# Strassen's products moved from the third matmul of a gated feed-forward to its first two, in half of the tokens

## Chip, core and metric

The kernel runs on one core of a Trainium2 chip. A core has five engines that run their own instruction streams and wait for each other through semaphores: TensorE (PE, matmuls, with weight loads counted apart as PEld), VectorE (DVE), ScalarE (ACT), GpSimd (POOL) and SyncE (SP, which only issues DMAs here). Matmul results land in PSUM, in banks of 512 float32 columns; everything else lives in SBUF. The metric is the device time of one execution in microseconds, as the median of several runs; lower is better.

## What is computed

```python
def _A_ref(x, wqkv, wo):            # B, S, D = 1, 2048, 512
    H = 32; Dh = D // H; W = 256
    qkv = (x @ wqkv).reshape(B, S, 3, H, Dh).transpose(2, 0, 3, 1, 4)
    q, k, v = qkv[0], qkv[1], qkv[2]
    scores = jnp.einsum("bhqd,bhkd->bhqk", q, k) * (Dh ** -0.5)
    mask = (idx[:, None] - idx[None, :] >= 0) & (idx[:, None] - idx[None, :] < W)
    p = softmax(jnp.where(mask, scores, -1e9))
    return einsum("bhqk,bhkd->bhqd", p, v) ... @ wo

def _B_ref(x, w1, w3, w2):          # F = 1792
    gate = jnp.einsum("bsd,df->bsf", x, w1)
    up = jnp.einsum("bsd,df->bsf", x, w3)
    return jnp.einsum("bsf,fd->bsd", silu(gate) * up, w2)

xn = layernorm(x)
return x + _A_ref(xn, wqkv, wo) * silu(_B_ref(xn, w1, w3, w2))
```

All inputs are float32.

## The kernel before

**Precision.** Each large matmul works in float16 with an operand split in a high and a low half, so a product is three matmuls: high by high, high by low, low by high. Splitting costs a cast (ScalarE or GpSimd) and a subtraction (GpSimd or VectorE). Weights are scaled by powers of two first.

**Tiles and units.** The 2048 tokens are four tiles of 512 (`t` from 0 to 3). Attention is done for 4 groups of 8 heads a tile, in two halves each, which gives 32 units. A unit has five batches of attention matmuls (`PLAN`): scores of the unit itself (`W`, line 720, followed by mask additions on VectorE, line 726, and an exponential on ScalarE, line 728), scores of a later unit for the row maxima (`M`, `X`, `N`, line 637, reduced on VectorE, line 650), and in the last batch the values (line 746). Between batches stand gaps, which are filled with dense matmuls.

**Dense work.** These are the projections of queries and keys (`project`, line 572), values (`value`, 539), the feed-forward, and the output product with the final gating (`total`, 1273). The feed-forward's hidden width of 1792 is 14 blocks of 128 (`f`). `gate_up(t, f)` makes 12 matmuls for gate and 12 for up, 512 columns each (line 1004), a Tanh on ScalarE (1018) and two VectorE products with PSUM (1021, 1025). In tiles 0 and 1 `down` (1224) multiplies by w2, in groups of 4, 4, 3 and 3 blocks, for 4 blocks of 128 tokens each, and adds groups in SBUF (1246).

In tiles 2 and 3 Down is a Strassen product: two blocks of `f` form a pair, tokens are split by parity and the output columns in half. `fold_weights` makes sums of quarters of w2 during tile 1 and stores them in `dFold`; `fold_first` and `fold_second` make sums of the hidden values on GpSimd and split them (1056 to 1084); `fold_down_piece` runs seven products of 256 columns (1144), and `unfold` adds them up (on GpSimd in tile 2, on VectorE in tile 3, lines 317 and 1176).

**Order.** `feed_forward` gives a list of pieces with costs (in units of one 512-column matmul). `more` takes from it so that each unit gets an equal share, and `spread` deals it over the gaps in proportion. Program order is kept on TensorE (`ORDERED`). For VectorE, ScalarE, GpSimd and SyncE the tables in `QUEUES` name the order of instructions by number, and `TURNS` lists pairs of a VectorE instruction that some GpSimd instruction has to wait for.

**Buffers.** Dense products use two PSUM banks in turn (`bank`, names m0 and m1). Scores have two buffers of two banks (`s`), and values and some scores share one of two banks (`po`). In SBUF 54 slots of 2 KB a partition are taken and given (`take`, `give`), and a slot given is reused.

Of the kernel before, what the change touches and what calls it, by code (L numbers as in the profile page):

```python
# [21 lines left out]
P = 128  # L22
# [16 lines left out]
XS = 2.0**10  # L39
# [4 lines left out]
HS = 2.0**4  # L44
# [7 lines left out]
SLOTS = 54  # L52
ORDERED = {ENGINE.PE}
GROUPS = ((0, 4), (4, 8), (8, 11), (11, 14))
FOLDS = ((0, 4), (4, 7))
FOLD_AT = (0, 1, 3, 5, 7, 9, 11)
SEVEN = (0, 6, 3, 4, 5, 1, 2)
KINDS = ((0,), (6, 3), (4, 5), (1, 2))
# [22 lines left out]
def tile_block(ctx: ExitStack, tc: tile.TileContext, x, wqkv, wo, w1, w3, w2, out):  # L81
# [17 lines left out]
    fpool = pool("fpool", 2)  # L99
    psm = pool("psm", 1, PSUM)  # L100
# [51 lines left out]
    open_bank = [0]  # L152

    def bank(shape, dtype=F32):

        open_bank[0] = b = 1 - open_bank[0]
        return psm.tile(shape, dtype, name=f"m{b}", tag=f"m{b}", bufs=1)
# [60 lines left out]
    dFold = dram.tile([len(KINDS), P, FB // 2, 2 * D], F16, name="dFold")  # L218
# [106 lines left out]

    WQ = {}
# [3 lines left out]
    def weights(name, w):  # L330
# [16 lines left out]
        def cut(apart=0):  # L347
            if name == "wo":

                made = [take(F16) for _ in range(NC)]  # L350
                hi, lo = ([m[:, k * D:(k + 1) * D] for m in made] for k in range(2))
            else:
                both = [const.tile([P, NC, D], F16, name=f"{name}{k}") for k in "hl"]
                hi, lo = ([b[:, c, :] for c in range(NC)] for b in both)
# [170 lines left out]
    def value(j, scores_bank=False):  # L525
# [4 lines left out]
        def part(half):  # L530
# [9 lines left out]
            if half:  # L540
                nc.scalar.activation(V[:, j % VB, 0:H * VW].rearrange("p (h w) -> p h w", w=VW)[:, :, 0:DH],
                                     pv.rearrange("p (h d) -> p h d", d=DH), AF.Copy, scale=sc["uv"])
        return opening([(6, lambda h=h: part(h)) for h in range(2)])
# [278 lines left out]
    sg_scale = const.tile([P, FB], F32, name="sgs")  # L822
    p13 = const.tile([P, FB], F32, name="p13")
# [16 lines left out]
    def measure(f, apart=0, until=8):  # L840
# [4 lines left out]
        def scale(s=None):  # L845
            pp = small.tile([P, 2, 2], F32, name="pp")
            pi = small.tile([P, 2, 2], F32, name="pi")
# [3 lines left out]
        def rest(pp, pi):  # L851
# [5 lines left out]
            def cut(i, k):  # L857
# [3 lines left out]
                split_pool(a[:, 0:D], a[:, D:], raws[i][k], pi[:, k, i:i + 1])  # L861
# [17 lines left out]
    def load_down(t, f):  # L879
        if t:  # L880
            WF[t, f][1] = b = take(F16)
            nc.sync.dma_start(b, dW2[f])
            return
# [3 lines left out]
    def measure_down(k, f):  # L887
# [18 lines left out]
        def rest(p2):  # L906
# [5 lines left out]
            if k:  # L912
                nc.vector.tensor_max(fold_q, fold_q, q)
            else:
                nc.vector.tensor_copy(fold_q, q)
# [14 lines left out]
            if f1 == FB:  # L930
                later(4, fold_scales)
        beside_scores(2, scale)

    fold_q = const.tile([P, 1], F32, name="fq")
    fold_down = const.tile([P, 1], F32, name="fd")
    fold_w = const.tile([P, FB], F32, name="fw")
    folded = []

    def fold_scales():

        folded.append(0)
        nc.vector.tensor_scalar(fold_down, fold_q, 1.0 / (HS * WS), None, op0=ALU.mult)
        nc.vector.reciprocal(fold_q, fold_q)
        nc.vector.tensor_scalar(fold_w, p13, fold_q, WS, op0=ALU.mult, op1=ALU.mult)

    def fold_weights(j):

        cell = {}
        l, r = slice(0, 256), slice(256, 512)
        sub = nc.gpsimd.tensor_sub  # L950

        def load():
            cell["raw"] = [take(F32) for _ in range(2)]
            for i, raw in enumerate(cell["raw"]):
                nc.sync.dma_start(raw, w2[(2 * j + i) * P:(2 * j + i + 1) * P, :])

        def sums():
            assert folded
            e, o = cell["raw"]
            for i, raw in enumerate((e, o)):  # L960
                nc.scalar.activation(raw, raw, AF.Copy, scale=fold_w[:, 2 * j + i:2 * j + i + 1])
            cell["z"] = z, y = [take(F32) for _ in range(2)]
            sub(z[:, l], e[:, r], e[:, l])
            sub(z[:, r], o[:, r], z[:, l])
# [801 lines left out]
```

## Time and profile before

| | |
|---|---|
| median of 3 runs | 799.32 us (798.89 to 800.25) |
| the profiled execution | 798.36 us, span 796.5 us |
| granted TensorE clock, mean | 0.999 |
| HBM read, written | 91.23 MB, 36.57 MB |

The span is the time from the first to the last instruction of the profiled execution. Times in the profile are in microseconds, or ns where it says so. A row of a group has the source line, the engine, the operation, output and inputs, shapes, and after x the count; then the busy time in all and the mean of one in ns; then the idle time ahead of them and who ended it. A row of the timeline has start, duration, and the same names. A row of a stretch has the busy time of PE, PEld, DVE, ACT and POOL with counts, the granted clock, the share of DMA time and GB/s. A matmul's own duration (380 ns at 512 columns) is longer than the distance from its start to the next one's, as matmuls overlap.

### The profile page before, as it was taken

Reading aid. Unit: us, or ns where it says so; the run is one execution under the profiler, and the core shown is the slowest. Engines: PE = TensorE matmul, PEld = TensorE weight load, DVE = VectorE, ACT = ScalarE, POOL = GpSimd, SP = SyncE. Lnnn points to the kernel's source line nnn. Section 1 sums busy time; section 2 is a strip of 40 time slices with the busy share of each in tenths; the row PEclk is TensorE's granted clock in tenths of the full one; section 3 lists DMA queues with packets and bytes.
Section 4 is the critical chain, followed back from the end, with each engine's and each line's share of the span. In section 5 each row is a group of like instructions: output and inputs, shape, how many; then the busy total and the mean of one; then the engine's idle time right before and its main releaser. Section 6 shows DMA issues by size and latency. Waiting matters only on the chain.

```text
span 796.5 us, 23974 instructions
## 1 busy us (share of the span) xinstructions
PE 788.6 (99%) x9181; PEld 403.3 (51%) x9181; DVE 616.6 (77%) x2005; ACT 396.1 (50%) x592; POOL 381.3 (48%) x746
## 2 busy tenths in 40 slices
PE   9999999999999999999999999999999999999997
PEld 4444455444544444444445454466544744466464
DVE  8689998977898678778978887766667877874437
ACT  8789958835365464344343444344434344444411
POOL 2254738742439463277422456330446277640770
PEclk9999999999999999999999999999999999999999
DMA  9878764747565574758465633765463553335431
GB/s 284 219 224 260 237 214 121 250 112 232 170 201 180 180 219 121 230 141 293 122 207 185 174 116 103 185 167 155 142 158 97 152 164 101 89 94 159 138 77 65
DMA packets 109858, 134.18 MB, mean 168 GB/s; under 512 B 18928, under 2 KB 64944, under 8 KB 109744
## 3 DMA queue, kind: packets, MB, share of 16 engines
q1 hardware_dynamic: 109456, 132.13, 55.9%
q8 instruction: 72, 1.18, 0.7%
q10 hardware_dynamic: 288, 0.52, 0.2%
q14 instruction: 42, 0.34, 0.1%
HBM read 91.23 MB, written 36.57 MB: 160 GB/s over the span
## 4 chain that ended last, share of the span: by engine, by line
PE 94%; DVE 3%; DMA 2%; ACT 1%; issue 0%; SPq 0%; DVEq 0%
PE m L1004 38%; PE po L746 9%; PE m L572 9%; PE m L1224 9%; PE m L1144 8%; PE s L720 6%; PE m L1273 5%; PE m L539 5%; PE s L637 3%; PE po L637 2%; DMA slot<-in_A_wqkv_dram 1%; DMA slot<-in_A_x_dram 0%; PE s L488 0%; DMA slot<-in_B_w_dram 0%; DVE junk L232 0%
## 5 line engine op out<-in xcount | busy, mean ns | idle before, releaser
L1004 PE MATMUL m<-XH,slot 128*128 128x512 f16 x896 | 267.3, 380 | 0.0
L728 ACT ACTIVATE pt<-s,es 128x1024 f32<-128x1024 f32 x152 | 167.2, 1114 | 142.7 <-DVE s L726 133.8
L1004 PEld LDWEIGHTS <-slot 128*128 128x128 f16 x1344 | 124.9, 98 | 154.1 <-issue 11.7
L1004 PE MATMUL m<-XL,slot 128*128 128x512 f16 x448 | 169.8, 379 | 0.0
L726 DVE TENSOR_TENSOR s<-s,MK 128x256 f32<-128x256 f32 (+2 forms) x280 | 120.5, 438 | 59.8 <-PE s L720 50.0
L650 DVE CUSTOM_DVE_ANT_0 junk<-s,MW 128x320 bf16<-128x320 f32 x276 | 122.0, 485 | 18.0 <-PE s L637 16.9
L317 POOL TENSOR_TENSOR slot<-slot,slot 128x256 f16<-128x256 f32 (+1 forms) x86 | 58.7, 699 | 75.1 <-ACT slot L1034 30.4
L323 POOL TENSOR_TENSOR slot<-slot,slot 128x128 f16<-128x128 f32 x168 | 66.7, 433 | 45.9 <-ACT slot L321 45.3
L1224 PE MATMUL m<-slot,slot 128*128 128x512 f16 x336 | 78.5, 380 | 0.0
L650 DVE CUSTOM_DVE_ANT_0 junk<-po,MW 128x320 bf16<-128x320 f32 x172 | 77.5, 484 | 0.0
L746 PE MATMUL po<-pt,V 64*32 64x320 f32 (+4 forms) x2880 | 77.2, 342 | 0.0
L1018 ACT ACTIVATE slot<-m,sgs 128x512 f32<-128x512 f32 x56 | 38.4, 686 | 69.2 <-PE m L1004 69.0
L572 PE MATMUL m<-XH,slot 128*128 128x512 f16 x240 | 70.8, 380 | 0.0
L1144 PE MATMUL m<-slot,slot 128*128 128x256 f16 x588 | 68.3, 273 | 0.0
L1059 POOL TENSOR_TENSOR slot<-slot,slot 128x256 f16<-128x256 f32 x98 | 65.1, 672 | 1.8
L1144 PEld LDWEIGHTS <-slot 128*128 128x128 f16 x588 | 56.2, 98 | 11.1 <-issue 2.7
L746 PEld LDWEIGHTS po<-pt,V 64*32 64x32 f32 x2880 | 50.3, 106 | 22.3 <-issue 0.8
L720 PE MATMUL s<-qa,KA 50*64 50x320 f16 (+3 forms) x1472 | 58.0, 259 | 0.0
L1021 DVE SCALAR_TENSOR_TENSOR slot<-slot,m 128x512 f32<-128x512 f32 x56 | 38.3, 683 | 25.2 <-ACT slot L1018 24.9
L572 PEld LDWEIGHTS <-slot 128*128 128x128 f16 x392 | 36.5, 98 | 42.0 <-issue 1.0
L720 PEld LDWEIGHTS <-KA 50*64 50x64 f16 x1472 | 30.0, 105 | 51.5 <-issue 40.0
L1025 DVE SCALAR_TENSOR_TENSOR slot<-m,slot 128x512 f32<-128x512 f32 x56 | 38.6, 689 | 18.7 <-PE m L1004 18.1
(194 smaller groups left out, 1126.2 us busy)
## 6 DMA issues: line engine op xcount, KB each, us to landing
slot<-dW SPq DMA_DIRECT2D x98, 256.0 KB
slot<-in_B_w_dram SPq DMA_DIRECT2D x56, 256.0 KB
slot<-dFold SPq DMA_DIRECT2D x48, 256.0 KB
dW<-slot SPq DMA_DIRECT2D x42, 256.0 KB
slot<-in_A_x_dram SPq DMA_DIRECT2D x30, 256.0 KB
KA<-dK SPq DMA_DIRECT2D x24, 288.0 KB
slot<-dWQ SPq DMA_DIRECT2D x24, 256.0 KB
qa<-dQ SPq DMA_DIRECT2D x30, 192.0 KB
```

What stands on the lines that cost most here:

```text
L317: op(out[:, c], a[:, c], b[:, c])
L323: nc.gpsimd.tensor_sub(lo[:, c:c + P], raw[:, c:c + P], hi[:, c:c + P])
L572: nc.tensor.matmul(cell["pp"][:, cols[n]], w[:, (a * NC + c) * P:(a * NC + c + 1) * P], b[:, c, cols[n]], start=n == 0 and (c, i) == parts ...
L650: nc.vector.tensor_tensor_reduce(out=junk[:, :n], in0=s[:, r, :n], in1=mask, scale=1.0, scalar=NEG, op0=ALU.add, op1=ALU.max, accum_out=M[ ...
L720: nc.tensor.matmul(s[64 * h:64 * h + 64, r, o:o + 64 * n], ka[rows, 2 * p + a, 64 * (m + 4):64 * (m + 5)], qa[rows, 2 * p + a, 64 * (m + k ...
L726: nc.vector.tensor_add(v, v, MK[:, kind, of:of + n, :].unsqueeze(1).to_broadcast([P, 2 * len(which), n, 64]))
L728: nc.scalar.activation(pt, s, AF.Exp, scale=es)
L746: nc.tensor.matmul(cell["po"][32 * i:32 * i + 32, h, 64 * (m + k):64 * (m + k + n)], V[64 * h:64 * h + 64, (4 * t + m // 2) % VB, hd * VW: ...
L1004: nc.tensor.matmul(cell[k], w[:, (a * NC + c) * P:(a * NC + c + 1) * P], b[:, c, :], start=c == 0 and i == 0, stop=c == NC - 1 and i == 2)
L1059: nc.gpsimd.tensor_sub(lo, view, hi)
L1144: nc.tensor.matmul(cell["ps"][:, c], made[:, f:f + P], wj[:, g:g + 256], start=j == j0 and c == 0 and n == 0, stop=j == j1 - 1 and n == 2, ...
L1224: nc.tensor.matmul(ps, hh[:, a * TW + b * P:a * TW + (b + 1) * P], w[:, c * D:(c + 1) * D], start=f == f0 and i == 0, stop=f == f1 - 1 and ...
```

## The change

Strassen's products are taken from Down and used for gate and up of tiles 2 and 3. Down of these tiles is done as in tiles 0 and 1. A pair of blocks `j` (blocks 2j and 2j+1) is one `quad`: the 2x2 split is over the two blocks, the two halves of the model width (256 each), and the two halves of the tile's tokens (256 each). Each of the seven products is 6 matmuls of 256 columns for gate and 6 for up, side by side in one bank (line 1113 in the new kernel). Four of them (p1, p6, p5, p3) add up in one bank, which keeps its sum from one to the next, so that ScalarE copies the sum after each; the other three go through the other bank and are added to a copy by VectorE. While the first bank is retained, `bank` hands out only the other one, to projections, values, Down and totals too.

Sums of quarters of w1 and w3 (`weight_sums`, GpSimd) are made during tile 1 and early in tile 2 from the weights read again, and stored in `dSum`; sums of quarters of the tokens (`token_sums`, GpSimd) near the end of tile 1 and of tile 2. The gating now reads copies in SBUF: product of gate and up on GpSimd, Tanh on ScalarE, one VectorE product, each in two halves of 256.

```diff
-SLOTS = 54
+SLOTS = 51
-FOLDS = ((0, 4), (4, 7))
+QUAD_FROM = 2
+QUAD_AT = ((1, 4), (1, 6), (1, 8), (1, 10), (1, 12), (2, 0), (2, 2))
+HALVES_AT = {2: (1, 11), 3: (2, 5)}
+FIRST_PAIR = 16
+REST = (19, )
+WEIGHTS = (0.9, 1, 1, 1.2, 0.9)
...
     def bank(shape, dtype=F32):
-        open_bank[0] = b = 1 - open_bank[0]
+        open_bank[0] = b = 1 - (open_bank[0] if retained[0] is None else retained[0])
...
-    def fold_weights(j):
-    def fold_first(t, j):
-    def fold_second(t, j):
-    def fold_down_piece(t, k, i):
-    def unfold(t):
+    def in_halves(made, raw):
+        for c in (0, 256):
+            nc.gpsimd.tensor_copy(made[:, c:c + 256], raw[:, c:c + 256])
+            nc.gpsimd.tensor_sub(made[:, 512 + c:768 + c], raw[:, c:c + 256], made[:, c:c + 256])
+    def weight_sums(j):
...
+        def sums(k):
+            a, b = cell[k]
+            add(b[:, r], b[:, l], b[:, r])
+            sub(b[:, l], a[:, l], b[:, l])
+            sub(a[:, l], b[:, r], a[:, l])
+            sub(a[:, r], a[:, r], a[:, l])
...
+    def quad(t, j):
...
+        def product(ps, w, x, first):
+            for k in range(2):
+                for c in range(2):
+                    for n, (a, b) in enumerate(((0, 0), (1, 0), (0, 1))):
+                        nc.tensor.matmul(ps[:, 256 * k:256 * k + 256], w(k, a, c), x(b, c), ...)
+        def copied(ps):
+            made = cpool.tile([P, 512], F32, name="copy")
+            nc.scalar.activation(made, ps, AF.Copy, scale=CS)
+            return made
+        def added(ps, other):
+            nc.vector.scalar_tensor_tensor(other, ps, CS, other, op0=ALU.mult, op1=ALU.add)
+            return other
+        def activated(f, half, made):
...
+            def tangent():
+                nc.gpsimd.tensor_mul(made[:, 256:512], made[:, 0:256], made[:, 256:512])
+                nc.scalar.activation(h, made[:, 0:256], AF.Tanh, scale=sg_apart[:, f:f + 1])
+            def gated():
+                nc.vector.scalar_tensor_tensor(h, h, 1.0, made[:, 256:512], op0=ALU.add, op1=ALU.mult)
+        def p1():
+            cell["a"] = bank([P, 512])
+            retained[0] = open_bank[0]
+            product(cell["a"], plain(0), tokens(0, 0), True)
+            cell["p1"] = copied(cell["a"])
+        def p2():
+            ps = bank([P, 512])
+            product(ps, plain(1), tokens(1, 0), True)
+            activated(e, 0, added(ps, cell["p1"]))
+        def p6():
+            product(cell["a"], summed_up(0, 0), token_sum(1, 256), False)
+            cell["u2"] = copied(cell["a"])
+        def p5():
+            product(cell["a"], summed_up(1, 256), token_sum(0, 0), False)
+            cell["v5"] = copied(cell["a"])
+        def p7():
+            cell["b"] = bank([P, 512])
+            product(cell["b"], summed_up(1, 0), token_sum(0, 256), True)
+            activated(o, 1, added(cell["b"], cell["v5"]))
+        def p3():
+            product(cell["a"], summed_up(0, 256), tokens(1, 256), False)
+            retained[0] = None
+            activated(e, 1, copied(cell["a"]))
+        def p4():
+            product(cell["b"], plain(2), token_sum(1, 0), False)
+            activated(o, 0, added(cell["b"], cell["u2"]))
...
+        return [pieces[:2], pieces[2:3], pieces[3:5], pieces[5:]]
```

From unit 16 on `by_gaps` deals the dense work. The four runs of a pair stand at fixed places: p1 and p2 in the last gap of a unit, p6 in the first gap of the next, p5 and p7 in the second, p3 and p4 in the third. Whole groups of the other dense work (a projection, a value product, a Down or total product) are dealt to the gaps that are left, at most one beside p6 and at most one in the second gap. There are 14 pairs for the last 16 units; unit 19 starts none. `QUEUES` and `TURNS` are new throughout.

In the next two blocks ScalarE's rows stand for one unit of tile 2: the middle of it, from the exponential of its first batch. Before, m_10031, m_10250 are gate products, m_10184 a projection, m_10305 a value product:

```order
L728 ACTIVATE pt<-s,es_1002 128x1024
L1056 CAST slot_10179<-slot_10124 128x256 x2
L728 ACTIVATE pt<-s,es_1002 128x1024
L587 ACTIVATE slot_10241<-m_10184 128x512
L1018 ACTIVATE slot_10266<-m_10250,sgs 128x512
L728 ACTIVATE pt<-s,es_1002 128x1024
L541 ACTIVATE V<-m_10305,uv 128x32x16
```

Now, where m_9939 is the bank retained by a pair and m_10020 a projection in the shared bank:

```order
L740 ACTIVATE pt<-s,es_1004 128x1024
L1119 ACTIVATE copy<-m_9939 128x512
L599 ACTIVATE slot_10033<-m_10020 128x512
L740 ACTIVATE pt<-s,es_1004 128x1024
L1119 ACTIVATE copy<-m_9939 128x512
L1136 ACTIVATE slot_10115<-copy,sga 128x256
L740 ACTIVATE pt<-s,es_1004 128x1024
L1119 ACTIVATE copy<-m_9939 128x512
```

A copy of the retained bank now stands between each two exponentials, and the next product of the pair waits for it.

VectorE's rows at the second and third batch of the same units, from the cast for the maxima on. Before, L1021 gates m_10250:

```order
L679 CAST mt<-s 32x128
L726 TENSOR_TENSOR s<-s,MK 128x4x64
L726 TENSOR_TENSOR s<-s,MK 128x2x2x64
L1021 SCALAR_TENSOR_TENSOR slot_10266<-slot_10266,m_10250 128x512
L650 ISA junk,M<-s,MW 128x320
L650 ISA M 128x1
```

Now, where m_10101 is the shared bank with p7:

```order
L691 CAST mt<-s 32x128
L1123 SCALAR_TENSOR_TENSOR copy<-m_10101,copy 128x512
L738 TENSOR_TENSOR s<-s,MK 128x4x64
L662 ISA junk,M<-s,MW 128x320
L662 ISA M 128x1
L738 TENSOR_TENSOR s<-s,MK 128x2x2x64
```

The sum for p7 now stands ahead of the third batch's masks, and a reduction between the two masks. The rows ahead of these, for the second batch, are a mask, the eviction of m_10020, a mask and four reductions.

VectorE's rows at the end of the program, while TensorE does its last products with w2. Before, L1160 evicts folded products, L317 and L1176 add them up, L811 makes the low half of the last attention output:

```order
L1160 SCALAR_TENSOR_TENSOR slot_12898<-m_13592,fd,slot_12898 128x512
L317 TENSOR_TENSOR slot_12898<-slot_12898,slot_12566 128x256 x2
L811 TENSOR_TENSOR slot_13589<-on,slot_13589 128x512
L1160 SCALAR_TENSOR_TENSOR slot_12925<-m_13612,fd,slot_12925 128x512
L317 TENSOR_TENSOR slot_12604<-slot_12604,slot_12898 128x256 x2
L1176 TENSOR_TENSOR slot_13653<-slot_12604,slot_12667 128x256
```

Now, where L1244 evicts plain Down and L823 is the old L811:

```order
L1266 SCALAR_TENSOR_TENSOR slot_14125<-slot_14125,slot_12572 128x512
L1266 SCALAR_TENSOR_TENSOR slot_14085<-slot_14085,slot_12808 128x512
L1244 SCALAR_TENSOR_TENSOR slot_12996<-m_14060,dsc,slot_12996 128x512
L1244 SCALAR_TENSOR_TENSOR slot_13225<-m_14071,dsc,slot_13225 128x512
L823 TENSOR_TENSOR slot_14057<-on,slot_14057 128x512
L1266 SCALAR_TENSOR_TENSOR slot_14106<-slot_14106,slot_13225 128x512
```

The small adds of the unfolding are gone from the end.

More of the change, by code (lines that the diff above doesn't have):

```diff
@@ L43 @@
 OS = 2.0**9
-HS = 2.0**4
+HS = 2.0**3
+CS = 2.0**-21
 TERMS = 3
@@ L347, in cut @@
         def cut(apart=0):
[L348 to L354, printed above, removed]
+            made = [take(F16) for _ in range(NC)]
+            SQ[name, "slots"] = made
+            hi, lo = ([m[:, k * D:(k + 1) * D] for m in made] for k in range(2))
             def one(c, raw):
@@ L930, in rest @@
             if f1 == FB:
-                later(4, fold_scales)
+                later(4, scales_apart)
         beside_scores(2, scale)
[L934 to L944, printed above, removed]
@@ L1166, in unfold @@
-    def unfold(t):
-        q = [QS7.pop((t, i)) for i in range(7)]
-        add = nc.gpsimd.tensor_add if t < NT - 1 else nc.vector.tensor_add
-        for b in range(4):
-            ACC[t, b] = take(F32)
-        def into(e, d, x, y):
-            for c in range(2):
-                h = slice(256 * c, 256 * c + 256)
-                add(ACC[t, 2 * c + e][:, 256 * d:256 * d + 256], x[:, h], y[:, h])
-        def first():
-            halves(add, q[5], q[5], q[0])
-            halves(add, q[6], q[6], q[5])
-        def second():
-            into(1, 0, q[6], q[3])
-            into(1, 1, q[6], q[4])
-        def third():
-            into(0, 0, q[0], q[1])
-            halves(add, q[5], q[5], q[4])
-            into(0, 1, q[5], q[2])
-            give(*q, after=30)
-            summed.update((t, b) for b in range(4))
-        if t == NT - 1:
-            first()
-            second()
-            third()
-        else:
-            for n, f in enumerate((first, second, third)):
-                later(1 + 4 * n, f)
@@ new lines, in tile_block, with token_sums, both, sums @@
+    HALF = {}
+    def token_sums(t):
+        assert turned[t] == 4
+        xh, xl = X[t]
+        add, sub = nc.gpsimd.tensor_add, nc.gpsimd.tensor_sub
+        l, r = slice(0, 256), slice(256, 512)
+        whole = [take(F32) for _ in range(NC)]
+        HALF[t] = [None] * NC
+        def both(c):
+            halves(add, whole[c], xh[:, c, :], xl[:, c, :])
+        def sums(c):
+            a, b = whole[c], whole[2 + c]
+            sub(a[:, l], a[:, r], a[:, l])
+            sub(a[:, r], b[:, r], a[:, r])
+            sub(b[:, r], b[:, r], a[:, l])
+            sub(b[:, l], b[:, l], b[:, r])
+        def cut(c):
+            HALF[t][c] = made = take(F16)
+            in_halves(made, whole[c])
+            give(whole[c], after=20)
+        n = 0
+        for f, cs in ((both, (0, 2, 1, 3)), (sums, (0, 1)), (cut, (0, 2, 1, 3))):
+            for c in cs:
+                later(n, lambda f=f, c=c: f(c))
+                n += 2
@@ L1312, in total_by_columns, with is_open, in_groups @@
         give(y, xr)
+    def is_open(pieces):
+        return bool(pieces) and hasattr(pieces[-1][1], "opens")
+    def in_groups(pieces):
+        groups = []
+        for piece in pieces:
+            if groups and is_open(groups[-1]):
+                groups[-1].append(piece)
+            else:
+                groups.append([piece])
+        return groups
     def feed_forward():
@@ L1574, in tile_block @@
     want = EARLY
+    coming = []
     for n, u in enumerate(units):
+        for f in ahead[n]:
+            later(5, f)
         if n == 0:
@@ L1597, in tile_block @@
         residual(NT - 1, b)
-    run(ffn)
+    run([piece for group in in_line + coming for piece in group])
     flush()
```

407 lines of the change are left out of this document (205 added, 202 removed), and 207 rows, old and new, of tables (QUEUES, TURNS).

## The prediction

> **What bounds the kernel now.** I read the page first, then who waits for whom on TensorE, then the counts by line and shape, then the order of time in one unit of tile 2.
>
> ```profile
> span 796.5 us, 23974 instructions
> PE 788.6 (99%) x9181; PEld 403.3 (51%) x9181; DVE 616.6 (77%) x2005; ACT 396.1 (50%) x592; POOL 381.3 (48%) x746
> PE 94%; DVE 3%; DMA 2%; ACT 1%; issue 0%; SPq 0%; DVEq 0%
> PE s L539 <- DVE wvl L312: 1.4, 2, 1.0
> PE m L1495 <- DVE onesb L183: 1.0, 1, 1.0
> PE m L468 <- DVE slot L452: 0.5, 1, 0.5
> PE s L265 <- DVE sb L242: 0.2, 1, 0.2
> 500.00:640.00 140.00, 140.00 (x1776) 79.58 (x1775) 101.31 (x324) 55.85 (x71) 52.89 (x90) 1.00 0.55 149
> 640.00:765.00 125.00, 125.00 (x1527) 67.01 (x1526) 81.20 (x234) 53.26 (x71) 73.31 (x123) 1.00 0.40 118
> ```
>
> TensorE's share of the chain is 94%. A busy 99% alone proves little, since ends of matmuls are modelled, but the four rows of waits are all that TensorE's matmuls have: 3.1 us, all in the first 30 us. In the stretches of tiles 2 and 3 (the last two rows) TensorE is never idle, at a granted clock of 1.00; VectorE is busy for 101.31 of 140 us (72%), ScalarE 40%, GpSimd 38 to 59%. So before the change a column streamed less is time saved, one for one, and the others have room on average.
>
> How long a column takes is read where matmuls of one kind stand alone, at the end:
>
> ```profile
> 762.30 0.60 PE L1004 MATMUL m<-XH,slot 128*128 128x512 f16 x2
> 767.49 13.92 PE L1144 MATMUL m<-slot,slot 128*128 128x256 f16 x126
> 781.25 7.93 PE L1273 MATMUL m<-slot,slot 128*128 128x512 f16 x36
> 789.02 2.78 PE L1307 MATMUL m<-slot,slot 128*128 128x256 f16 x24
> ```
>
> From start to start: 36 matmuls of 512 columns in 789.02 - 781.25 = 7.77 us, 215.8 ns each; 126 of 256 columns, each with new weights, in 781.25 - 767.49 = 13.76 us, 109.2 ns each. Two halves cost 1.2% more than one whole.
>
> **The matmuls that go and come.**
>
> ```profile
> L1004 PE MATMUL m<-XH,slot 128*128 128x512 f16 x896 | 267.3, 380 | 0.0
> L1004 PE MATMUL m<-XL,slot 128*128 128x512 f16 x448 | 169.8, 379 | 0.0
> L1224 PE MATMUL m<-slot,slot 128*128 128x512 f16 x336 | 78.5, 380 | 0.0
> L1144 PE MATMUL m<-slot,slot 128*128 128x256 f16 x588 | 68.3, 273 | 0.0
> ```
>
> Gate and up have 896 + 448 = 1344 matmuls over four tiles; the half of tiles 2 and 3 goes: 672 x 215.8 ns = 145.0 us. The folded Down of these tiles goes too: 588 x 109.2 ns = 64.2 us. Plain Down, as tiles 0 and 1 have it, comes: 336 x 215.8 ns = 72.5 us. The Strassen products come: 2 tiles x 7 pairs of blocks x 7 products x 12 = 1176 matmuls of 256 columns, 128.4 us. Sum: 128.4 + 72.5 - 145.0 - 64.2 = **-8.3 us**. The count of batches, and so of the breaks between dense work and attention, stays. If a short run costs what 24 matmuls in 2.78 us say (115.8 ns, with the fill of the last), the 588 matmuls more of this width cost 3.9 us more; I take 109.2, as the products stand inside long runs.
>
> [...]
>
> **The other engines' work.**
>
> ```profile
> L1025 DVE SCALAR_TENSOR_TENSOR slot<-m,slot 128x512 f32<-128x512 f32 x56 | 38.6, 689 | 18.7 <-PE m L1004 18.1
> L1021 DVE SCALAR_TENSOR_TENSOR slot<-slot,m 128x512 f32<-128x512 f32 x56 | 38.3, 683 | 25.2 <-ACT slot L1018 24.9
> L1246 DVE SCALAR_TENSOR_TENSOR slot<-m,dsc,slot 128x512 f32<-128x512 f32 x24 | 17.8, 744 | 4.1 <-PE m L1224 4.1
> L1160 DVE SCALAR_TENSOR_TENSOR slot<-m,fd,slot 128x512 f32<-128x512 f32 x14 | 10.5, 748 | 7.3 <-PE m L1144 7.3
> L1018 ACT ACTIVATE slot<-m,sgs 128x512 f32<-128x512 f32 x56 | 38.4, 686 | 69.2 <-PE m L1004 69.0
> L1059 POOL TENSOR_TENSOR slot<-slot,slot 128x256 f16<-128x256 f32 x98 | 65.1, 672 | 1.8
> L1058 POOL CAST slot<-slot 128x256 f16<-128x256 f32 x56 | 22.5, 408 | 1.3 <-DVE slot L1268 0.7 <-DVE NM L667 0.2
> q1 hardware_dynamic: 109456, 132.13, 55.9%
> ```
>
> VectorE loses 28 each of L1025 and L1021, the 14 of L1160 and 16 small adds of the last unfolding (0.42 us), 55.6 us; it gains 24 evictions of plain Down at 0.744, 42 sums of a product with a copy, priced by the same row, and 56 half-width gatings (some 0.45 us by half a wide row and its start): 74.3 us. That is +18.7 us, 81% of the new span. ScalarE gains 56 copies of products at 0.69, 56 half-width Tanh and 28 scalings of weights against what folding took: some +42 us, 56%. GpSimd gives up all folding (about 200 us by counts at 0.67 to 0.75 and 0.41) and gets weight sums, token sums and gating for about 220. Some 43 transfers of 256 KB more, 11 MB on 132, lift the queue's 55.9% to about 60%. By these sums alone all of it lies beside TensorE's work, and I cost it at nothing. The cover is thin only where order binds.
>
> **Where it binds: the two short gaps of a unit.** While a pair of blocks is open, one of the two banks for dense work stays with it (products 1, 6, 5, 3), and all else shares the other. And p5 with p7, and p3 with p4, stand alone between batches: 24 half-wide matmuls, 2.62 us.
>
> ```profile
> 576.61 0.41 PE L720 MATMUL s<-qa,KA 50*64 50x320 f16 x8
> 577.07 0.90 DVE L726 TENSOR_TENSOR s<-s,MK 128x256 f32<-128x256 f32 x2 [0.97 <-PE s L720]
> 577.23 0.39 PE L539 MATMUL m<-wvh,XH 128*128 128x512 f16 x1
> 578.09 1.12 ACT L728 ACTIVATE pt<-s,es 128x1024 f32<-128x1024 f32 x1 [0.69 <-DVE s L726]
> 578.47 0.48 DVE L650 CUSTOM_DVE_ANT_0 junk<-s,MW 128x320 bf16<-128x320 f32 x1
> 578.88 0.49 DVE L650 CUSTOM_DVE_ANT_0 junk<-s,MW 128x320 bf16<-128x320 f32 x1
> 582.51 0.64 PE L720 MATMUL s<-qa,KA 50*64 50x320 f16 x24
> 587.21 0.47 PE L637 MATMUL s<-KA,qa 48*32 48x320 f16 x16
> ```
>
> Now batches start 5.9 and 4.7 us apart (576.61, 582.51, 587.21). A batch itself takes 577.23 - 576.61 = 0.62 us and 0.1 of break, so the new period of the two short gaps is 0.72 + 2.62 = 3.34 us. I walk VectorE's row in the order shown above from the second batch of a unit on, with t = 0 where that batch starts. First mask at 0.46 (577.07 - 576.61); masks and reductions 0.41 each from start to start (578.88 - 578.47); wide evictions 0.61 to 0.69. Mask, eviction of the group that shares the bank, mask, four reductions, the cast for the maxima (0.2), the sum for p7 (0.66): VectorE is done with the second batch at 4.4. The third batch began at 3.34 and its mask could have begun at 3.8, so VectorE is 0.6 late. Mask, reduction, mask: 5.62. The exponential starts 0.12 later and takes 1.12: 6.86. The fourth batch's scores want that buffer at 2 x 3.34 = 6.68. TensorE stands for about **0.2 us**; with the printed means in place of the pitches it is 0.5, and in a unit where the shared group is evicted by ScalarE it is nothing. Queued behind that matmul on TensorE stands everything dense. The fourth gap (two 2.6 us groups) then gives VectorE its time back, so lateness doesn't add up from unit to unit. The other waits of that kind have more room: p4 needs the sum for p7, done at 4.4, and starts at 3.34 + 0.72 + 1.31 = 5.4; p3 needs ScalarE's copy of p5, which stands behind one exponential, done near 3.9, and starts at 4.06. That one is almost as tight. Bounds: 0 and 0.5 us for each of 14 pairs, 0 to 7 us; I take 0.2, the walk by pitches, nearest to the rows: **+2.8 us**.
>
> **Data on time.** The first p5 of tile 2 needs the token sums, about 90 GpSimd instructions after the last reader of their slots, 56.5 us by the rows above; TensorE has 79 us of work between the two. Cost nothing, 22 us of cover, less what GpSimd waits for DMAs.
>
> **The end.**
>
> ```profile
> 762.41 0.69 DVE L760 COPY os<-po 128x512 f32<-128x512 f32 x1 [1.79 <-DMA slot<-dFold]
> 776.03 1.41 POOL L317 TENSOR_TENSOR on<-on,rb 128x256 f32<-128x256 f32 x2 [1.06 <-DMA rb<-de]
> 778.98 0.68 DVE L811 TENSOR_TENSOR slot<-on,slot 128x512 f16<-128x512 f32 x1
> ```
>
> The last head group's normalised output is ready at 779.66, 17.4 us after the last dense gap begins (762.30). There the old kernel puts 18.95 us of dense work, the new one eight groups of 9 matmuls, 15.5 us, and the product that needs the low half comes 11 matmuls on, at 17.9. So the shorter tail stays covered by half a microsecond. What goes there is in the counts already.
>
> **Sum.** -8.3 + 2.8 = -5.5 us. The profiled execution took 798.36 us, its span 796.5 and 1.86 around it; the median shown is 799.32, 0.96 above. On the profiled run: 792.9; on the median, which is compared: **793.8**. A measurement of this kernel tells about 0.2% from no change, 1.6 us.
>
> **Rivals.**
> 1. VectorE is late by the printed means, 0.5 us a pair: 799.32 - 8.3 + 7.0 = 798.0. For it: 72% busy before and the walk's 0.2 to 0.5. Against: units whose shared group is evicted by ScalarE have slack. Chance 0.17.
> 2. Slower: the shared bank. If evictions stand behind reductions, p5, p4 or the group behind p6 waits on the bank as well. Break-even is 8.3 / 14 = 0.59 us a pair; one more eviction late (0.69) on top of 0.2 gives 0.89, 12.5 us: 803.5. For it: p3's 0.16 us of margin above. Against: the waits overlap, since a late TensorE gives the others time. Chance 0.14.
> 3. Token sums late at tile 2 by a quarter of their cover, 5 us once: 798.8. Chance 0.05.
> 4. The clock. [...] Chance 0.02.
> 5. That it doesn't do what it says: 256-column matmuls would have to take 336 x 215.8 / 588 = 123.3 ns for no gain; 126 in a row took 109.2. Within case 1's time, no chance of its own.
>
> The forecast, 791 to 796.5, has the other 0.62. **Faster** by over 0.2% (below 797.7): 0.62 and half of case 1, 0.70. **Within**: the other half and most of case 3, 0.14. **Slower** (above 800.9): 0.16. The range goes from 790.0, no stall at all (791.0) and the end a little shorter, to 800.5, both upper bounds (7.0 us of stalls and half of the 3.9 for short runs); above it lie cases 2 and 4.
>
> **What will show it.** L1113 at 109 ns from start to start in runs of 24; waits of TensorE for ScalarE's exponential at L732 near 0.2 us in the fourth batch of a unit; span near 791. A wait at L1113 for L1123 or L1119 speaks for case 2, a single long one at the first token sums for case 3, a clock below 1.00 for case 4. The prediction is wrong if TensorE's waits in tiles 2 and 3 sum to over 8 us, or if the first 500 us, in which TensorE's work stays the same, move by more than 1 us.

## The result, and the profile after

The change makes the kernel slower. Its median is 809.06 us (804.34 to 813.65, six runs) against 799.27 us (798.14 to 800.25) for the kernel before on the same chip, a ratio of 1.012 with a 95% interval of 1.0076 to 1.0165. The prediction, 793.8 us with a range of 790.0 to 800.5, misses it by 15 us, on the other side. The profiled execution took 812.34 us, the second longest of the six, with a span of 810.6, 14.1 more than before; the medians differ by 9.8.

The page's first lines after, its chain by engine and its queue, in the order in which they were shown of before:

```profile
span 810.6 us, 24698 instructions
PE 788.5 (97%) x9433; PEld 431.3 (53%) x9433; DVE 617.6 (76%) x2037; ACT 430.9 (53%) x656; POOL 399.3 (49%) x761
q1 hardware_dynamic: 129712, 142.23, 58.7%
PE 55%; DMA 9%; SPq 4%; POOL 2%; DVE 2%; issue 1%; ACT 1%; POOLq 0%; DVEq 0%; ACTq 0%
```

Busy times give no alarm: VectorE has 1 us more than before (the sum had said 18.7; the busy time counts rows that overlap once, and the durations of all its rows, added up, grow by 13.2), ScalarE 34.8 more (42), the queue is at 58.7% (60). But TensorE's share of the chain has fallen from 94% to 55%. Who TensorE waits for (us in all, times, the longest), the first six rows:

```profile
PE m L1113 <- DMA slot<-dW: 4.6, 1, 4.6
PE m L1113 <- DMA slot<-dSum: 4.1, 1, 4.1
PE m L1113 <- ACT copy L1119: 3.1, 1, 3.1
PE s L649 <- ACT pt L740: 2.4, 4, 0.7
PE m L1540 <- DVE onesb L188: 1.0, 1, 1.0
PE m L1222 <- DVE slot L1244: 0.6, 2, 0.3
```

Three single waits, at the products' line, make 11.8 us. Line 649 waits for exponentials, 2.4 us in all, but two of its four waits, 1.4 us together, come at 250 us, before the first product. Where the loss happens is read from stretches of the trace (length, then the busy time of PE, PEld, DVE, ACT and POOL with counts, granted clock, DMA share, GB/s). First the kernel before:

```profile
400.00:500.00 100.00, 100.00 (x1346) 48.94 (x1344) 82.28 (x258) 39.65 (x51) 42.87 (x73) 1.00 0.55 160
500.00:600.00 100.00, 100.00 (x1210) 54.70 (x1209) 68.93 (x225) 41.86 (x54) 33.81 (x58) 1.00 0.59 158
```

and the changed one:

```profile
0.00:400.00 400.00, 396.14 (x4360) 188.87 (x4361) 319.32 (x1142) 235.65 (x377) 192.28 (x421) 1.00 0.61 182
400.00:500.00 100.00, 89.86 (x1236) 55.35 (x1235) 76.95 (x244) 48.88 (x69) 65.04 (x116) 0.95 0.74 220
500.00:600.00 100.00, 96.72 (x1242) 57.04 (x1239) 73.63 (x232) 51.43 (x72) 66.91 (x111) 0.98 0.64 200
600.00:760.00 160.00, 159.26 (x2212) 103.79 (x2212) 119.20 (x376) 80.14 (x117) 55.20 (x85) 1.00 0.50 148
```

TensorE's loss is in 400 to 600 us, the end of tile 1 and the first half of tiles 2 and 3; 10.1 us of idle lie before 500 us and 3.3 behind. From 600 to 760 us, with the same products in the same short gaps, it is idle for 0.74 us. In the stretch of the loss VectorE does as much as before (150.6 us in the two rows, against 151.2), while GpSimd goes from 42.87 to 65.04 us and then from 33.81 to 66.91, and the DMA engines from 0.55 to 0.74 and from 0.59 to 0.64. Over the whole run both hardly moved (GpSimd from 381.3 to 399.3 us, the queue from 55.9% to 58.7%).

Now the first of the three waits, on the timeline of TensorE (start, length, what, and in brackets the idle time and who ended it):

```profile
424.66 2.53 PE L758 MATMUL po<-pt,V 64*32 64x256 f32 x96
431.74 0.61 PE L1113 MATMUL m<-XH,slot 128*128 128x256 f16 x2 [4.55 <-DMA slot<-dW]
...
436.97 0.45 PE L732 MATMUL s<-qa,KA 50*64 50x256 f16 x8
```

and the chain of waits that leads to it, in order of time:

```profile
424.01 1.26 POOL slot L322 x2
425.27 0.33 POOL slot L997
425.60 6.10 DMA slot<-dW
431.70 0.04 issue
431.74 5.30 PE m L1113 x24
```

The weights of the first product go into a slot that held raw weights for a weight sum. GpSimd, busy for 15.08 of the 15.60 us from 410.00 on, releases it at 425.60; the load takes 6.10 us more, and TensorE stands from 427.2 on. When it starts, 24 matmuls take 436.97 - 431.74 = 5.23 us, 218 ns each, and the granted clock is 0.50. Later, from 602.87 to 605.59, 24 of them take 2.72, at 1.00.

The second wait is a load in SyncE's queue behind a store of keys (SPq is SyncE's own time), which waits for VectorE:

```profile
459.19 0.69 DVE copy L1123
459.88 0.62 DVE s L738
460.50 0.29 SPq L608
...
460.88 3.69 DMA slot<-dSum
464.57 0.05 issue
464.62 1.46 PE m L1113 x6
```

The third is ScalarE's: its cast at line 1191 waits 7.89 us for a slot that an output store still reads (`DMA out_dram<-slot`, 4.46 us, issued only at 553.15: it stood in SyncE's order behind six transfers of the attention and two loads for the products), and the copy of a product out of the bank, line 1119, stands behind it in ScalarE's order. So it isn't the shared bank that failed there, but a slot.

To see where the 14.1 us come from, each TensorE row of both traces was given the time from its start to the next row's start, less that row's wait:

| us | before | after | e3_all (below) |
|---|---|---|---|
| gate and up, plain | 298.8 | 149.4 | 149.3 |
| Down (before: with the folded one) | 141.2 | 149.5 | 149.6 |
| Strassen products | | 136.4 | 134.2 |
| queries and keys | 85.5 | 87.6 | 85.1 |
| waits | 2.1 | 16.9 | 10.8 |

Waits bring +14.8, the matmuls -4.7 (with what the slower clock cost the products), the slower clock on the projections of queries and keys +2.1, and all other kinds some 2.

### The profile page after: what moved, and what is told of

It reads as the page before. It is cut to its first block, busy times and chain, and to the rows that moved or that the text cites. A ratio compares the mean times of both kernels' runs of the same rounds, so it can differ in the third digit from the quotient of the medians.

```text
span 810.6 us, 24698 instructions
## 1 busy us (share of the span) xinstructions
PE 788.5 (97%) x9433; PEld 431.3 (53%) x9433; DVE 617.6 (76%) x2037; ACT 430.9 (53%) x656; POOL 399.3 (49%) x761
## 3 DMA queue, kind: packets, MB, share of 16 engines
q1 hardware_dynamic: 129712, 142.23, 58.7%
## 4 chain that ended last, share of the span: by engine, by line
PE 55%; DMA 9%; SPq 4%; POOL 2%; DVE 2%; issue 1%; ACT 1%; POOLq 0%; DVEq 0%; ACTq 0%
PE m L1113 13%; PE m L1222 12%; PE m L962 6%; PE po L758 6%; PE m L584 5%; PE m L1271 4%; PE s L732 3%; PE m L549 2%; PE s L649 2%; DMA slot<-dW 1%; DMA KA<-dK 1%; SPq L782 1%; DMA out_dram<-slot 1%; DMA slot<-dSum 1%; SPq L695 1%
## 5 line engine op out<-in xcount | busy, mean ns | idle before, releaser
L1222 PE MATMUL m<-slot,slot 128*128 128x512 f16 x672 | 154.6, 379 | 1.4 <-DVE slot L1244 0.6
L322 POOL TENSOR_TENSOR slot<-slot,slot 128x256 f16<-128x256 f32 (+1 forms) x136 | 91.3, 692 | 131.1 <-ACT slot L988 72.4
L962 PE MATMUL m<-XH,slot 128*128 128x512 f16 x448 | 133.7, 380 | 0.0
L1113 PEld LDWEIGHTS <-slot 128*128 128x128 f16 x1176 | 112.0, 99 | 36.3 <-issue 10.0
L1222 PEld LDWEIGHTS <-slot 128*128 128x128 f16 x672 | 63.2, 98 | 76.9 <-issue 5.4
L962 PEld LDWEIGHTS <-slot 128*128 128x128 f16 x672 | 62.4, 98 | 77.2 <-issue 5.5
L1113 PE MATMUL m<-slot,slot 128*128 128x256 f16 x672 | 81.5, 275 | 7.1 <-DMA slot<-dSum 4.1
L962 PE MATMUL m<-XL,slot 128*128 128x512 f16 x224 | 84.9, 379 | 0.0
L1135 POOL TENSOR_TENSOR copy<-copy 128x256 f32<-128x256 f32 x56 | 40.8, 737 | 79.7 <-DVE copy L1123 65.9
L584 PE MATMUL m<-XH,slot 128*128 128x512 f16 x240 | 72.8, 389 | 0.0
L338 POOL TENSOR_TENSOR slot<-slot,slot 128x128 f16<-128x128 f32 x112 | 45.0, 439 | 47.4 <-ACT slot L335 42.9
L1119 ACT ACTIVATE copy<-m 128x512 f32<-128x512 f32 x56 | 33.2, 592 | 64.5 <-PE m L1113 64.5
L1113 PE MATMUL m<-XH,slot 128*128 128x256 f16 x336 | 59.2, 280 | 4.6 <-DMA slot<-dW 4.6
L584 PEld LDWEIGHTS <-slot 128*128 128x128 f16 x392 | 37.3, 100 | 43.5 <-issue 4.2
```

The costliest lines, as they stand in the source:

```text
L322: op(out[:, c], a[:, c], b[:, c])
L338: nc.gpsimd.tensor_sub(lo[:, c // 2, at], raw[:, c * P:(c + 1) * P], hi[:, c // 2, at])
L584: nc.tensor.matmul(cell["pp"][:, cols[n]], w[:, (a * NC + c) * P:(a * NC + c + 1) * P], b[:, c, cols[n]], start=n == 0 and (c, i) == parts ...
L962: nc.tensor.matmul(cell[k], w[:, at:at + P], b[:, c, :], start=c == 0 and i == 0, stop=c == NC - 1 and i == 2)
L1113: nc.tensor.matmul(ps[:, 256 * k:256 * k + 256], w(k, a, c), x(b, c), start=first and k == 0 and c == 0 and n == 0, stop=k == 1 and c == 1 ...
L1135: nc.gpsimd.tensor_mul(made[:, 256:512], made[:, 0:256], made[:, 256:512])
```

## Experiments

The theories at the start: **A**, three late transfers and the clock behind them are the whole loss; **B**, the short gaps (VectorE, the shared bank); **C**, the transfers and GpSimd are too full as a whole, and stops come back elsewhere. The later ones, **G**, **Q**, **S** and **T**, are told in the expectations where they come in.

### Removing the three stops

e1_swap lets two loads change places, so that the first product's weights get a slot that is free 13 us earlier:

```diff
-pieces += [(0, lambda i=i: load_quad(QUAD_FROM, 0, i)) for i in (0, 1, 3, 4, 5, 6)]
+pieces += [(0, lambda i=i: load_quad(QUAD_FROM, 0, i)) for i in (4, 1, 3, 0, 5, 6)]
```

> The two loads of the first Strassen pair that change places are those of the weights of its first product (p1) and of one weight sum that is needed two gaps later: p1's weights get the buffer that is free 13 us earlier. Theory A (three late transfers, each followed by matmuls at a lower granted clock, make the whole loss): the row 'L1113 <- DMA slot<-dW: 4.6' goes, the 24 matmuls behind it take 2.7 us and not 5.3, the other two long rows (4.1 and 3.1) stay; 4.6 + 2.6 = 7.2 us less, a median near 802. Theory B (the loss is spread over the 14 pairs: VectorE and the shared bank in the short gaps): the first stop may go, but its 24 matmuls are slow anyway and the time stays above 807. Theory C (GpSimd and the queue are too full as a whole): the stop of 4 us or more comes back at the next load, and the time stays at 809 +- 2.

e2_sp moves two transfers in SyncE's table: the second pair's load ahead of the store of keys, and the output store twelve places forward.

```diff
     assert len(line) == len(made)
+    if engine == ENGINE.SP:
+        for a, b in ((556, 555), (680, 668)):
+            line.insert(b, line.pop(a))
```

> Two transfers move ahead in SyncE's order: the weight sum that the second pair waits for goes in front of a store of keys, and one output store of tile 1 goes twelve places forward. Theory A: the rows of 4.1 us (dSum) and 3.1 us (ACT copy) go, with them the slower clock behind both (granted clock 1.00 in 450-475 and 550-575 us), the first of 4.6 stays; 7.2 us of waits and 3 to 4 us of slow clock less: a median near 798.5. Theory B: above 806. Theory C: the two stops come back at other transfers, 809 +- 2.

e3_all has both edits.

> Both edits together. Theory A: no wait of TensorE over 1 us in tiles 2 and 3, granted clock 1.00 there, 11.8 us of waits and about 6.5 us of slow clock less than the changed kernel: a median near 791 (789 to 795), so faster than the kernel before by about 8 us, which is the sum of the matmuls that the prediction made. Theory B: near 803 to 806, slower than before. Theory C: new stops of several us at other buffers, 800 to 809.

Measured: e1_swap 807.15 us, ratio 1.0106 [1.0088, 1.0123]; e2_sp 804.74, 1.0081 [1.0055, 1.0107]; e3_all 803.20 (800.27 to 804.97), 1.0054 [1.0037, 1.0072]. The gains from 809.06 are 1.9, 4.3 and 5.9 us, and the last is a third of the 18 that A promised. Only its interval is clear of the changed kernel's [1.0076, 1.0165]; the other two overlap it, so that the parts add up is not shown. (The kernel before, run again beside each set, had medians from 798.77 to 799.27, so half a microsecond between sets means nothing.) In the trace of e1_swap the first product no longer waits, but the second waits 1.6 us for its own weights, and the other two stops stay at 3.3 and 2.4. TensorE's waits in e3_all, the three longest rows and those of the old stops:

```profile
PE s L649 <- ACT pt L740: 2.1, 2, 1.4
PE m L1113 <- DMA slot<-dSum: 1.8, 1, 1.8
PE m L1222 <- DVE copy L1123: 1.6, 1, 1.6
...
PE m L1113 <- ACT copy L1119: 0.8, 1, 0.8
PE m L1113 <- DMA slot<-dW: 0.7, 1, 0.7
```

The three stops have shrunk from 11.8 us to 3.3, and the clock is 1.00 in both stretches; but smaller stops at other places have come. This trace is of the fastest of the six runs; in the other five the mean granted clock is 0.995 to 0.998 (1.000 here). Longer stops in them would fit that, but are not shown. In the stretch of the loss:

```profile
400.00:500.00 100.00, 93.47 (x1322) 57.05 (x1328) 81.17 (x253) 51.97 (x74) 72.26 (x127) 1.00 0.76 230
500.00:600.00 100.00, 99.00 (x1367) 60.88 (x1352) 76.42 (x243) 51.63 (x73) 67.31 (x111) 1.00 0.69 211
```

A as the whole cause falls: 6.5 us of idle are left in 400 to 500 us where before had none, behind transfers, VectorE and ScalarE in turn. That is C's picture; which of its parts counts, the next kernels ask.

### What the clock cost

```diff
             retained[0] = open_bank[0]
+            if (t, j) == (QUAD_FROM, 0):
+                for _ in range(21):
+                    nc.tensor.matmul(cell["a"], identh, X[t][0][:, 0, :], start=True, stop=True, ...)
             product(cell["a"], plain(0), tokens(0, 0), True)
```

> Nothing is moved. 21 matmuls of 128x512 whose result is overwritten stand ahead of the first product of the first Strassen pair, into its own bank: 21 x 0.216 = 4.5 us, as long as the first stop. Theory A (the clock falls because TensorE stood still): the products' weights land as late as before, so the stop itself stays (filled), but the 24 matmuls behind it take 2.7 us and not 5.3: 2.6 us less, a median near 806.5, the granted clock 1.00 in 430 to 440 us. If the clock falls for another reason, the 24 matmuls still take about 5.3 us and the time stays at 809; if the stop is not the transfer's, the 4.5 us come on top, 813.

Measured: 808.41 us, ratio 1.0124 [1.0108, 1.0141]. The timeline of TensorE at the first stop:

```profile
426.79 4.71 PE L1153 MATMUL m<-XH,identh 128*128 128x512 f16 x21
431.34 0.38 PE L1113 MATMUL m<-XH,slot 128*128 128x256 f16 x2
...
434.05 0.41 PE L732 MATMUL s<-qa,KA 50*64 50x256 f16 x8
```

The 24 matmuls now take 434.05 - 431.34 = 2.71 us, and the granted clock from 425 to 450 us is 1.00, where the changed kernel has 0.86. So TensorE standing still for 4.55 us is what makes them slow there, and 2.5 us are saved on the spot. The time gains nothing that can be told from noise (0.65 us by the medians, none by the ratios, 1.0124 and 1.0120): in this trace the waits for ScalarE's copies sum to 4.0 us over two stops, where there was one of 3.1, and all waits with the 4.5 us of filling to 17.7, against 16.9. That what TensorE gains at one late transfer it loses at the next is a reading of this one trace, and not shown by more.

### Which work sets the pace

Three kernels on top of e3_all make one kind of work lighter without moving an instruction. They leave out most of that work, so their feed-forward of tiles 2 and 3 is not the one asked for; they are there for their time alone.

```diff
 # e5_thin_sums, in weight_sums
+            l, r = slice(0, 32), slice(256, 288)
             add(b[:, r], b[:, l], b[:, r])
 # e8_thin_dve
-            nc.vector.scalar_tensor_tensor(other, ps, CS, other, op0=ALU.mult, op1=ALU.add)
+            nc.vector.scalar_tensor_tensor(other[:, 0:64], ps[:, 0:64], CS, other[:, 0:64], ...)
-                nc.vector.scalar_tensor_tensor(h, h, 1.0, made[:, 256:512], ...)
+                nc.vector.scalar_tensor_tensor(h[:, 0:32], h[:, 0:32], 1.0, made[:, 256:288], ...)
 # e9_thin_loads, in load_quad; the products then read QW[t, j, i][:, 0:P] for every block
-            src = dW1[f, :, :, at:at + 512].rearrange("k p x -> p k x")
+            src = dW1[f, :, :, at:at + 64].rearrange("k p x -> p k x")
-            nc.sync.dma_start(made, dSum[(i - 3) // 2, (i - 3) % 2, j])
+            nc.sync.dma_start(made[:, 0:128], dSum[(i - 3) // 2, (i - 3) % 2, j, :, 0:128])
```

> On top of the two edits of e3_all (803.2 us, 10.8 us of idle TensorE against 2.1 in the kernel before, 6.2 of them between 425 and 475 us). GpSimd's four additions and subtractions of each weight sum work on 32 columns instead of 256, so the weight sums hold wrong numbers; about 56 instructions fall from 0.73 to some 0.2 us, 30 us of GpSimd less, 12 us of them between 400 and 475 us, where it was busy 58 of 75 us. Theory G (GpSimd's backlog in the handover from tile 1 to tile 2 is what makes buffers and loads late): idle TensorE in 425 to 475 us falls from 6.2 to under 2.5, the time to 798 to 799. Theory Q (the transfers and SyncE's order are late by themselves): idle changes by less than 1.5 us, 802 to 804. Theory B (VectorE and the shared bank in the short gaps): no change, 803.

> On top of e3_all. VectorE's two instructions per product half (the addition out of the bank and the gating) work on 64 and 32 columns instead of 512 and 256, so tiles 2 and 3 of the feed-forward hold wrong numbers: 56 x 0.5 and 56 x 0.2 us, some 35 us of VectorE less in tiles 2 and 3, and the shared bank is left 0.5 us earlier. Theory B: the waits for VectorE, for the copies out of the bank and for ScalarE's exponentials (2.1 + 1.6 + 0.8 us in e3_all) go and the time falls to 797 or below. Theories G and Q: these instructions are late because of buffers and loads, not for their own length: 1 to 2 us less at most, 801 to 803.

> On top of e3_all. The seven loads of a Strassen pair bring 32 KB each instead of 256 KB (the products use the same 128 columns throughout, so tiles 2 and 3 of the feed-forward are wrong); the number, order and place of the transfers stay, 98 x 224 KB = 22 MB of 142 MB go. Theory Q, as far as bytes are the limit: the share of the DMA engines in 425 to 475 us falls from 0.8 to about 0.6, loads land in 3 us and not 5, idle there falls from 6.2 to under 2.5 and the time to 798 to 799. Theory G, or SyncE's order without regard to bytes: less than 2 us, 801 to 803. Theory B: no change.

Measured: e5_thin_sums 801.26 us, ratio 1.0025 [1.0011, 1.0040]; e8_thin_dve 800.97, 1.0023 [1.0004, 1.0041]; e9_thin_loads 797.20 (792.90 to 799.34), 0.9972 [0.9955, 0.9988]. From e3_all that is -1.9, -2.2 and -6.0 us. The bytes of the products' loads are the largest part: these 98 transfers of 256 KB, cut to 32 KB with their number and order unchanged, decide between slower and faster than before. It is not SyncE's time for issuing them: in 450 to 475 us SyncE's instructions fill 22.1 of 25 us in e3_all and 22.3 in e9_thin_loads. The stretch of the loss in e9_thin_loads:

```profile
400.00:500.00 100.00, 95.07 (x1351) 57.86 (x1357) 83.29 (x259) 52.74 (x74) 73.01 (x128) 1.00 0.65 183
500.00:600.00 100.00, 99.32 (x1351) 61.28 (x1336) 75.73 (x247) 52.50 (x74) 66.22 (x110) 1.00 0.49 137
```

The DMA share falls to 0.65 and 0.49, and the idle in the first stretch from 6.5 to 4.9 us; this trace is of that kernel's slowest run and e3_all's of its fastest, so the profiles show less of the gain than the medians. Between 425 and 475 us the idle falls from 6.35 to 3.63 us, not below 2.5 as Q had it, though the time fell by more than Q said. B's 797 or below for thinner VectorE work did not come; its 2.2 us and the 1.9 of e5_thin_sums have intervals that just overlap e3_all's, so either can be nothing, and by the ends of the intervals VectorE's length is worth about 5 us at most. G's 4 to 5 us did not come either (idle between 425 and 475 us is 6.14 us there, where G had under 2.5).

Two more: all three lightenings at once, and buffers of their own for the thin loads.

```diff
 # e11_own, on top of e9_thin_loads
-    cpool = pool("cpool", 7)
+    cpool = pool("cpool", 5)
+    qwpool = pool("qwpool", 2)
-        QW[t, j, i] = made = take(F16)
+        QSL[t, j, i] = take(F16)
+        QW[t, j, i] = made = qwpool.tile([P, 128], F16, name=f"qw{i}", tag=f"qw{i}", bufs=2)
```

> e3_all with the three lightenings at once: weight sums of 32 columns on GpSimd, 64 and 32 columns in VectorE's two instructions of the products, 32 KB in each of the products' loads (tiles 2 and 3 of the feed-forward are wrong). If the extra work of GpSimd, VectorE and the transfers is the whole of what e3_all still loses (10.8 us of idle TensorE against 2.1 before), the time is TensorE's own sum, 791 to 793, the idle 3 to 4 us. If order and buffers keep a part (thinner work does not bring a buffer free earlier when it waits for a store or a place in SyncE's order), 794 to 796.

> e9_thin_loads (797.2 us), with 14 small buffers of their own for the products' loads, two for each of the seven; the rows of the buffer book stay taken, so every other tile keeps its place. The space comes from two of the seven buffers of the copies out of the bank (5 instead of 7). Theory S (51 buffers are too few: a load waits until the last holder of its buffer is stored or cut): idle in 400 to 500 us falls from 5 to under 2 us and the time to 793 to 795. If the loads were no longer held by their buffers in e9_thin_loads, nothing changes (796 to 798); if the two copies that are taken away are missed, it grows by 1 to 3 us, with waits for ACT copy.

Measured: e10_all_thin 795.13 us (793.13 to 795.70), ratio 0.9944 [0.9924, 0.9965]; e11_own 796.67, 0.9974 [0.9960, 0.9988]. The three together give 8.1 us of the 10.1 that they give apart. What TensorE still waits for in e10_all_thin, the longest four:

```profile
PE s L732 <- ACT pt L740: 2.1, 2, 1.2
PE s L649 <- DVE XL L507: 1.2, 1, 1.2
PE m L1541 <- DVE onesb L188: 1.0, 1, 1.0
PE s L265 <- DVE sq L441: 1.0, 1, 1.0
```

Some 7.4 us of waits are left against 2.1 before, most at places that are none of the products' (exponentials, tokens, small sums; the first wait at a product's line has 0.4 us). The time is in the 794 to 796 of that expectation's second half; that order and buffers are what keeps these waits is its argument, and not shown. The gain over e9_thin_loads, 2.1 us, has overlapping intervals. Once loads are light, S finds nothing: their own buffers change the time by 0.5 us, within the intervals, and idle in 400 to 500 us is 3.95 us, not under 2. Whether heavy loads wait for buffers as such stays open, since no run tried it.

### Order in SyncE's queue, and no order at all

e12_hoist extends e2_sp's list of moves by 17, the first of them (547, 542) and (555, 551).

> On top of e3_all, 17 more loads of the products move up to five places forward in SyncE's order (about 2 us of issues), all those between the second pair and the end of tile 3's third that wait for no engine; nothing else changes. Theory Q by order (urgent loads stand behind less urgent transfers): waits for slot<-dSum and slot<-dW go below 1 us in all, the time from 803.2 to 798 to 800. Theory Q by bytes (the transfers as a whole are too many for the stretch, e9_thin_loads): what moves forward pushes others back; waits move to qa, rb or the x tiles and the time stays at 801 to 805.

Measured: 808.72 us, ratio 1.0117 [1.0097, 1.0137], 5.5 us slower than e3_all. It misses both expectations. TensorE's longest waits now:

```profile
PE m L584 <- DVE copy L1123: 2.8, 1, 2.8
PE m L1222 <- DVE copy L1123: 2.3, 2, 1.2
PE m L1113 <- DMA slot<-dSum: 2.2, 1, 2.2
PE m L1113 <- ACT copy L1119: 1.7, 1, 1.7
PE s L649 <- DVE XL L507: 1.4, 1, 1.4
```

A weight sum is waited for as long as before (2.2 us, 1.8 in e3_all), and VectorE and ScalarE are late in more places. Moving these loads ahead made other work late by more than it gained; that any other order would do so too is not shown.

e6_untabled and e7_untabled_before leave out `queue(tc, engine, order)` for all engines; the pairs of `TURNS` stay.

> The changed kernel without the four tables of order: each of the four engines takes its instructions in the order in which the program issues them. To be read against e7_untabled_before. Theories Q, G and S (the extra loads, stores and sums crowd the handover in either order): 5 to 15 us slower than e7, both above 800. Rival T (the products themselves gain, and only the tables of the changed kernel are badly chosen): 5 to 10 us faster than e7, as TensorE's sum says.

> The kernel before without its four tables, the mark against which e6_untabled is read. All theories: slower than 799.3, 805 to 830, by what the order by hand is worth there.

Measured: 874.99 us (ratio 1.0947 [1.0909, 1.0986]) and 847.16 us (1.0599 [1.0583, 1.0615]). In program order the change costs 27.8 us, more than the 5 to 15 expected. T's forecast fails: without any table the products do not come out ahead. That a better table exists isn't excluded by it, and e3_all, two of whose three moves are in SyncE's order, shows that the order chosen cost something. The order by hand is worth 48 us to the kernel before and 66 to the changed one. The two longest rows of TensorE's waits in e6_untabled are both for exponentials, which stand late on ScalarE there:

```profile
PE s L732 <- ACT pt L740: 15.8, 6, 8.2
PE s L649 <- ACT pt L740: 15.3, 11, 8.9
```

No version that computes the whole result was faster than the kernel before; e3_all is the best of the changed ones.

## Why the prediction was wrong, step by step

**The step that failed** is "By these sums alone all of it lies beside TensorE's work, and I cost it at nothing". The sums over the run came near and had the wrong extent. The 43 transfers more and GpSimd's trade of folding for weight and token sums were added up over the run, 55.9 to about 60% and about 200 against 220 us. But folding had stood late and the new work stands early: in 400 to 600 us GpSimd rises from 76.7 to 132.0 us, and in 600 to 760 us it falls from 88.6 to 55.2. The share of the DMA engines rises from 0.55 to 0.74 in 400 to 500 us and from 0.59 to 0.64 in the next 100. Raw weights, stored sums and products' loads meet the end of tile 1, its output stores and tile 3's tokens there. The prediction had read its stretches of tiles 2 and 3 from 500 us on; but in the trace before, tile 2's gate products start at 418 us, and 10.1 us of idle lie between 400 and 500. e9_thin_loads shows that the bytes of the products' loads alone are worth 6.0 us; the two edits of e3_all, which free a slot and two places in SyncE's order, 5.9 more; GpSimd's and VectorE's lengths together about 2 beyond that (797.20 to 795.13, with overlapping intervals). These sizes go from 809.06 to 795.13, 1.3 us from the forecast.

**Data on time** looked for one late thing, the token sums, and gave them 22 us of cover. They were on time: no wait stands at the first p5. The loads of the weights were not asked about, neither which slot each would get and who releases it, nor what stands before it in SyncE's order. The rows for that were to be had before: the order of SyncE's transfers, and the 56.5 us of GpSimd work that the prediction itself put ahead of tile 2.

**The matmuls** came out near the sum, in part by luck, since two terms were too small by 4.5 and 5.8 us and cancel: gate and up 149.5 us less (145.0 predicted), Down 8.4 more (8.3), the products 134.2 (128.4), read in e3_all at full clock; -6.9 for -8.3. A product's matmul takes 134.2 / 1176 = 114 ns, and 24 of them with the break behind them take 2.72 us. The 115.8 ns that the prediction had named for short runs was the nearer row, and the halves of gate and up, runs of 12 wide ones, were dearer than 215.8 by their breaks too (149.5 / 672 = 222.5 ns).

**The two short gaps.** Predicted +2.8 us (0 to 7) of waits for exponentials at line 732. No such wait came: the row has 2.4 us at line 649, two waits at 250 us, before any pair, and two, 1.0 us together, at 480 and 481 us, behind a whole group of the output product and not in a short gap. 600 to 760 us, nearly half of the pairs' time, have 0.74 us of idle for all causes. So this term was too large, and the slower time has to come from elsewhere. Cases 1 and 2, the lateness by the printed means and the shared bank, did not happen: the one long wait at 1113 for 1119 had its cause in a slot. e8_thin_dve puts all of it at 2.2 us, by the ends of the intervals at 0 to 5. (The two upper bounds that the range names add up to 800.0 and not 800.5, which changes nothing.)

**The end** was covered, as said: no wait stands in the last 40 us, and TensorE's last group starts 810.6 - 804.06 = 6.5 us before the end of the span, where it was 796.5 - 789.02 = 7.5.

**The clock** (case 4, its chance of 0.02 the author's estimate) did fall, but behind single long waits (0.50 behind the one of 4.55 us) and not in the short gaps, where it stays at 1.00 (600 to 760 us). Against e3_all, whose trace has the full clock, its direct price is 2.1 us on queries and keys (before: 85.5) and 2.2 on products (136.4 to 134.2). By the granted clock, 0.95 and 0.98 in the two stretches, 5 and 2 us of full-clock time are missing, a part of them while TensorE stood; so 4.3 is the lower of two estimates. The prediction's own test, waits in tiles 2 and 3 of over 8 us, is what happened. Its other test failed as well, and its premise with it: TensorE's work does not stay the same in the first 500 us, as the first product starts at 431.74, and from 400 to 500 us TensorE loses 10.1 us. Only the first 400 us stay the same, within 0.7 us (396.81 to 396.14 us of TensorE).

## What to carry to other kernels

Add up what a change puts on queues and helpers by stretch, not over the run: 18 us more of GpSimd in all were 55 us more in one quarter of the time. For each new load ask three things before costing it at nothing: who last used its buffer, what stands ahead of it in the queue that issues it, and how full the DMA engines are just then. And a stop that was removed paid here only as far as the next one: cutting three stops from 11.8 us to 3.3 brought 5.9.

## What the runs showed that was not expected

**After a single wait of 2 to 3 us matmuls can take twice their time.** In e8_thin_dve, after 2.42 us of idle (start, length, what, wait):

```profile
457.02 1.46 PE L1113 MATMUL m<-slot,slot 128*128 128x256 f16 x6 [2.42 <-DMA slot<-dSum]
458.27 1.06 PE L584 MATMUL m<-XH,slot 128*128 128x512 f16 x2
459.13 0.63 PE L584 MATMUL m<-XL,slot 128*128 128x512 f16 x1
```

From 458.27 to 459.13 two matmuls of 512 columns take 430 ns each, twice the usual 215.8, and the granted clock from 450 to 475 us is 0.93. The same followed waits of 2.01 us (e5_thin_sums, 430 us, granted clock 0.93 from 425 to 450 us) and 4.55 (the changed kernel, 0.50 as said); it did not follow 2.40 us in e1_swap at 554 us (1.00 from 550 to 575 us), nor 2.13 in e5_thin_sums at 459 (1.00 from 450 to 475 us). So the length of the wait alone does not decide it in these traces, and what does is not shown.

**The changed kernel spreads.** Six of its runs lie 9.3 us apart, as many of the kernel before 2.1. Why is not shown: with the light loads of e9_thin_loads ten runs still lie 6.4 us apart.
